# First chunk of a gated linear attention loaded in long runs, with block-masked cumulative sums and single units in the first layer

## The chip, the cores and the metric

The kernel runs on one core of a Trainium2 chip. The metric is the device time of that core in microseconds (us). A run of a new kernel is set beside runs of the kernel before on the same chip.

## The reference

```
# q, k, v, alpha: 4 batches x 8 heads x 768 tokens x 48, float32
for t in range(S):
    state = alpha[t] * state + outer(k[t], v[t])      # 48 x 48 per batch and head
    y[t]  = q[t] @ state
x = y as 3072 tokens x 384
h = x @ w_in                                          # 384 -> 2048
out = gelu_tanh(h) @ w_out                            # 2048 -> 384, float32
```

The recurrence is done in six chunks of 128 tokens: within a chunk by masked scores, between chunks by the state. A "unit" is one batch's chunk (128 tokens, all 8 heads), and a "pair" is two units. Pairs 0 and 1 are chunk 0, pair 2 is the first pair of chunk 1, and so on to pair 11.

## The kernel before

A small scheduler in Python knows a cost for each task, lays the tasks out in time, and emits them in that order. So each engine has a fixed order, and every number in the table `W` can change it. Parts that matter (cuts marked with `...`):

```python
SPLIT = (2,)                      # pair 2 is loaded in two halves
LOADS = ("0", "1", "in 0", ..., "in 3", "out 0", ..., "out 3", "2", "3", ..., "11")

def load(self, n, c, i, lo=0, hi=2):       # one strip: 128 tokens on partitions
    ...
    src = self.src[n][2*i+lo:2*i+hi].rearrange("b h s d -> s (b h) d")[c*C:(c+1)*C]
    (nc.sync if e == "SP" else nc.gpsimd).dma_start(u[n][:, lo:hi]..., src)   # runs of 48 floats

def cum(self, u, lo, hi):                  # cumulative log decay: one matmul a unit
    for i in range(lo, hi):
        nc.tensor.matmul(cum[:, i, 0:H*D], self.ut_h, la[:, i, :, 0:D], ...)
        ...                                # 4 matmuls of 1 column: the chunk's total

def layer1(self, f, c, lo, hi, nt):        # a pair: 256 columns a matmul
    for j in range(self.NKT):
        self.nc.tensor.matmul(h, self.w_in[:, j, nt*C:(nt+1)*C], self.xT[c][:, j, lo:hi]..., ...)

for m in range(len(self.BLOCKS)):          # order of the two layers
    layer1(m)
    if m:
        for j in (0, 1) if m == 1 else (m,):
            layer2(j)
```

With that order TensorE does the first layer of both pairs of chunk 0 before any of the second layer. Where the scheduler expects TensorE to sit idle, it puts in matmuls on zeros ("idle<-zero"). They are meant to keep TensorE's clock up.

## Time and profile before

| | before |
|---|---|
| time, median of 3 (lowest to highest) | 192.81 us (192.59 to 192.82) |
| span of the profiled run | 191.0 us |
| TensorE busy, of it on zeros | 181.4 us, 11.2 us |
| first layer starts | 21.77 us |
| k of pair 2 (second half) has landed | 41.64 us |
| TensorE ends its last matmul | 187.33 us |

In a line of the timeline come the start, the length, engine, source line, operation, "out<-in", the shape and the count. In brackets stands how long the engine was idle before it and what it waited for. In the chain of waits each line is one step of the path that ended last. A "DMA" step is time spent on a transfer. The lines themselves stand in the prediction below.

### The profile page before, as it was taken

How to read it: one execution, taken by the hardware profiler on the slowest of the kernel's cores; microseconds unless marked ns; L12 is line 12 of the kernel's file. 1: busy time of each engine (PE TensorE's matmuls, PEld its weight loads, DVE VectorE, ACT ScalarE, POOL GpSimd, SP SyncE). 2: the span in 40 equal slices, each digit the busy share in tenths (PEclk: the TensorE clock that was granted, in tenths of full speed). 3: DMA queues.
4: the chain of work that ended last, by engine and by line, in shares of the span. 5: the costliest groups of instructions: out<-in, count | busy, mean ns of one | idle time of the engine just before them, and what ended most of it. 6: DMA issues, size and time to landing. Idle time of an engine off the chain costs nothing.

```text
span 191.0 us, 4655 instructions
## 1 busy us (share of the span) xinstructions
PE 181.4 (95%) x1919; PEld 131.8 (69%) x1922; DVE 111.2 (58%) x232; ACT 135.8 (71%) x300; POOL 63.8 (33%) x67
## 2 busy tenths in 40 slices
PE   5887899999999999999999999999999999999992
PEld 1343688656687787786786786786786786785860
DVE  7268650279695794793793883892892950850000
ACT  2544989743868878878778788788688788881931
POOL 7993433896547564655502400000000000000000
PEclk9999999999999999999999999999999999999999
DMA  6999999999999999999998770200200201101101
GB/s 129 181 179 171 207 202 228 182 180 227 249 210 182 164 241 178 181 253 173 187 246 165 152 185 0 84 2 3 82 0 6 80 3 40 42 3 43 45 13 70
DMA packets 38005, 24.68 MB, mean 129 GB/s; under 512 B 27968, under 2 KB 34624, under 8 KB 37984
## 3 DMA queue, kind: packets, MB, share of 16 engines
q0 software_dynamic: 32464, 19.27, 72.5%
q1 hardware_dynamic: 5520, 5.11, 9.1%
q8 instruction: 15, 0.25, 0.6%
q14 instruction: 6, 0.05, 0.1%
HBM read 25.17 MB, written 4.72 MB: 156 GB/s over the span
## 4 chain that ended last, share of the span: by engine, by line
PE 75%; DMA 17%; POOL 4%; issue 1%; DVE 1%; ACT 1%; POOLq 0%; DVEq 0%
PE acc L412 29%; PE hT L398 28%; DMA k<-in_k_dram 9%; DMA w_out<-in_moe_w_out_dram 8%; PE qkT_ps L289 5%; PE at L325 3%; PE yps L374 2%; PE yps L371 2%; PE kv L342 2%; PE xT_ps L388 2%; PE cum L252 2%; POOL q L220 1%; PE cum L254 1%; POOL a L220 1%; POOL k L220 1%
## 5 line engine op out<-in xcount | busy, mean ns | idle before, releaser
L404 ACT ACTIVATE gT<-hT 128x256 bf16<-128x256 f32 x192 | 64.5, 385 | 16.3 <-PE hT L398 15.6
L398 PE MATMUL hT<-xT,w_in 128*128 128x256 bf16 x576 | 71.6, 273 | 0.1
L412 PE MATMUL acc<-w_out,gT 128*128 128x384 bf16 x384 | 68.6, 326 | 0.0
L398 PEld LDWEIGHTS <-w_in 128*128 128x128 bf16 x576 | 53.6, 98 | 8.1 <-issue 0.4
L412 PEld LDWEIGHTS <-gT 128*128 128x128 bf16 x384 | 35.9, 98 | 20.2
L332 DVE TENSOR_TENSOR atm<-at,ut 128x512 bf16<-128x512 f32 x48 | 30.9, 686 | 4.8 <-PE at L325 3.2
L278 DVE TENSOR_TENSOR qp<-q,b 128x768 bf16<-128x768 f32 (+1 forms) x13 | 11.6, 896 | 33.2 <-ACT b L270 33.2
L419 ACT COPY ot<-acc 128x384 f32<-128x384 f32 x16 | 7.7, 478 | 19.0 <-PE acc L412 19.0
L220 POOL DMA_DIRECT2D a<-in_alpha_dram x12 | 13.3, 1110 | 15.3 <-ACT la L241 8.8
L220 POOL DMA_DIRECT2D q<-in_q_dram x13 | 14.6, 1122 | 11.5 <-DVE qp L278 3.6
L220 POOL DMA_DIRECT2D v<-in_v_dram x13 | 14.4, 1111 | 8.0 <-PE hT L398 1.9
L303 DVE COPY qkT<-qkT_ps 128x1024 bf16<-128x1024 bf16 (+1 forms) x22 | 13.8, 663 | 5.5 <-PE qkT_ps L289 5.5
L220 POOL DMA_DIRECT2D k<-in_k_dram x13 | 14.5, 1113 | 7.3 <-DVE xT L392 2.0
L198 ACT ACT_TABLE_LOAD x10 | 12.8, 1283 | 0.9 <-PEq L627 0.7
L241 ACT ACTIVATE la<-a 128x768 f16<-128x768 f32 (+1 forms) x13 | 10.3, 794 | 3.9 <-DMA a<-in_alpha_dram 3.7
L404 ACT ACT_TABLE_LOAD x10 | 12.8, 1283 | 0.2
L270 ACT ACTIVATE b<-cum 128x768 bf16<-128x768 f32 (+1 forms) x13 | 9.9, 762 | 4.1 <-PE cum L254 3.7
L207 PE MATMUL idle<-zero 128*128 128x512 bf16 x31 | 11.2, 483 | 1.4 <-DVE zero L594 1.2
L359 DVE TENSOR_TENSOR st<-stmp,bend 64x192 bf16<-64x192 f32 x32 | 11.3, 353 | 2.1 <-ACT gT L404 0.5
L278 DVE TENSOR_TENSOR kp<-k,binv 128x768 bf16<-128x768 f32 (+1 forms) x15 | 11.7, 792 | 0.6 <-DMA k<-in_k_dram 0.5
L392 DVE COPY xT<-xT_ps 128x384 bf16<-128x384 bf16 x24 | 8.5, 354 | 5.0 <-PE xT_ps L388 5.0
L357 DVE TENSOR_TENSOR stmp<-kv,st 64x192 f32<-64x192 f32 x32 | 11.2, 351 | 0.2
(43 smaller groups left out, 166.8 us busy)
## 6 DMA issues: line engine op xcount, KB each, us to landing
out_dram<-ot SPq DMA_DIRECT2D x24, 192.0 KB, 4.0
q<-in_q_dram POOLq DMA_DIRECT2D x11, 384.0 KB, 13.1
k<-in_k_dram POOLq DMA_DIRECT2D x11, 384.0 KB, 13.0
a<-in_alpha_dram POOLq DMA_DIRECT2D x10, 384.0 KB, 13.0
v<-in_v_dram POOLq DMA_DIRECT2D x11, 192.0 KB, 12.6
w_in<-in_moe_w_in_dram POOLq DMA_DIRECT2D x4, 384.0 KB, 11.8
w_out<-in_moe_w_out_dram POOLq DMA_DIRECT2D x4, 384.0 KB, 15.2
a<-in_alpha_dram SPq DMA_DIRECT2D x1, 384.0 KB, 4.1
```

Source lines behind the costliest of these rows:

```text
L198: nc.scalar.add_instruction(mybir.InstLoadActFuncSet(name=nc.get_next_instruction_name(), act_func_set_id=i, engine=mybir.EngineType.Activ ...
L207: self.nc.tensor.matmul(ps, self.zero[:, 0:self.C], self.zero, start=True, stop=True)
L220: (nc.sync if e == "SP" else nc.gpsimd).dma_start(u[n][:, lo:hi].rearrange("t b h d -> t (b h) d"), src)
L241: self.nc.scalar.activation(u["la"][:, lo:hi, :, 0:self.D], u["a"][:, lo:hi], AF.Ln)
L278: self.nc.vector.tensor_tensor(u[n + "p"][:, lo:hi, :, 0:self.D], u[n][:, lo:hi], u["b" if n == "q" else "binv"][:, lo:hi], op=ALU.mult)
L303: self.copy(e)(t, u.pop(("T_ps", i, which)))
L332: self.nc.vector.tensor_tensor(u["atm", i][:, o], u["at", i][:, o], self.ut[:, None, :].to_broadcast([self.C, self.H // 2, self.C]), op=AL ...
L357: nc.vector.tensor_tensor(s[ps], acc, old[ps, :, fs], op=ALU.add)
L359: nc.vector.tensor_tensor(new[ps, :, fs], acc, u["bend"][ps, i, :, None].to_broadcast([64, H // 2, D]), op=ALU.mult)
L398: self.nc.tensor.matmul(h, self.w_in[:, j, nt * self.C:(nt + 1) * self.C], self.xT[c][:, j, lo:hi].rearrange("p g t -> p (g t)"), start=j ...
L404: return lambda e: self.nc.scalar.activation(self.gT[c % self.NG][:, nt, lo * self.C:hi * self.C], f.pop(("h", c, lo, nt)), AF.Gelu_apprx_ ...
L412: self.nc.tensor.matmul(f["acc", c, b], self.gT[c % self.NG][:, nt, b * self.C:(b + 1) * self.C], self.w_out[:, nt, :], start=nt == 0, sto ...
```

## The change

The intent is an earlier start. Chunk 0's a, q and k come in runs of four tokens (768 B in place of 192 B), so that they take less transfer time. Tokens then lie four to a partition, so cumulative sums have to be put together from blocks, and k has to be put back in token order for the matmul that forms the state (`kv`). Core of the diff:

```diff
-    SPLIT = (2,)
-    EARLY = (0, 1)
-    LOADS = ("0", "1", "in 0", ...
+    SPLIT = ()
+    LOADS = ("v0", "v1", "in 0", ...
+    R = 4
+    def load_first(self, n, b):
+            src = self.src[n][b, :, 0:self.C].rearrange("h (j r) d -> j h (r d)", r=R)
+            dst = self.first[n].rearrange("(j b) h r d -> b j h (r d)", b=4)[b]
+            (self.nc.sync if e == "SP" else self.nc.scalar).dma_start(dst, src)
+    def cum_first(self, g, p):             # 16 matmuls of 96 columns and 4 of 4, for 2 heads of all units
+            for r in range(R):
+                for s in range(R):
+                    nc.tensor.matmul(cum[:, r*n:(r+1)*n], self.ut_blk[s > r], la[:, s, :, 0:D], ...)
+    def shift(self, b):                    # k back to token order: 16 copies of 32 KB within SBUF
+            for r in range(R):
+                self.nc.sync.dma_start(self.k_first[:, b].rearrange("(j r) h d -> r j h d", r=R)[r],
+                                       self.kp_first.rearrange("(j b) r h d -> b j r h d", b=4)[b, :, r])
...
+        load(["gate"], "POOL", 100, 0, lambda e: self.nc.gpsimd.tensor_copy(self.gate, self.first["q"][:, 0, 0, 0:1]))
+        loads["gate"][0].deps += loads["q", "first"]      # no load from GpSimd until q has landed
...
+        layer1(0, 0, 1, 0, 12)             # units 0 and 1 singly, 128 columns
+        layer1(0, 1, 2, 0, 12)
+        layer1(0, 0, 1, 12)
+        layer1(0, 1, 2, 12)
+        decays(2)                          # cumulative sums of a later pair
+        layer2(0, 0, 2)
+        layer1(0, 2, 4)                    # units 2 and 3 as a pair, after the second layer of 0 and 1
+        decays(3)
+        layer2(0, 2, 4)
```

There are also new numbers in `W` (among them `l1_1=680` for six single matmuls). One buffer is given up (`ot` 6 to 5).

## The prediction

> **What bounds the kernel now.** I read the page first (busy shares, then the 40 slices), then the chain of work that ended last in order of time, then a table of windows, then GpSimd's timeline for the landings of the loads.
>
> ```profile
> PE 181.4 (95%) x1919; PEld 131.8 (69%) x1922; DVE 111.2 (58%) x232; ACT 135.8 (71%) x300; POOL 63.8 (33%) x67
> PE   5887899999999999999999999999999999999992
> DMA  6999999999999999999998770200200201101101
> L207 PE MATMUL idle<-zero 128*128 128x512 bf16 x31 | 11.2, 483 | 1.4 <-DVE zero L594 1.2
> ```
>
> TensorE is busy nearly always from about 30 us, but its 181 us include 11.2 us of matmuls on zeros that only keep the clock up. The DMA engines are full for the first half. So the end is set by TensorE, and a gain can only come from time in which TensorE has no real work. The windows show where that is (columns: window, its length, then busy us of PE, PEld, DVE, ACT, POOL, clock, DMA share, GB/s):
>
> ```profile
> 0.00:21.77 21.77, 16.54 (x141) 8.11 (x144) 13.18 (x40) 10.14 (x17) 16.24 (x24) 1.00 1.24 170
> 21.77:34.00 12.23, 12.23 (x133) 10.46 (x131) 4.85 (x11) 11.60 (x34) 5.17 (x6) 1.00 1.28 213
> 34.00:50.50 16.50, 15.82 (x157) 9.77 (x157) 10.75 (x23) 9.53 (x20) 12.48 (x12) 1.00 1.35 211
> 50.50:187.40 136.90, 136.79 (x1494) 103.41 (x1493) 82.45 (x160) 104.14 (x232) 29.93 (x26) 1.00 0.67 107
> ```
>
> The first layer starts at 21.77; before it TensorE has 16.54 - 10.05 (zeros, same windows for that tile) = 6.5 us of real work. From 34 to 50.5 about 1.9 us are lost. From 50.5 on nothing is. The chain says what leads up to the dense part:
>
> ```profile
> 17.35 15.28 DMA w_out<-in_moe_w_out_dram
> 32.63 0.62 issue
> 33.25 8.39 DMA k<-in_k_dram
> 41.73 0.56 DVE kp L278
> 42.29 0.48 DVE qp L278
> 42.82 0.62 PE qkT_ps L289 x8
> ```
>
> Until 41.64 us the chain is a queue of transfers: all of chunk 0, all weights, then the first strips of chunk 1. GpSimd's waits give the landings one after the other:
>
> ```profile
> 20.08 0.90 POOL L220 DMA_DIRECT2D a<-in_alpha_dram  x1 [0.65 <-DMA w_in<-in_moe_w_in_dram]
> 22.82 0.89 POOL L220 DMA_DIRECT2D q<-in_q_dram  x1 [1.84 <-DMA w_in<-in_moe_w_in_dram]
> 24.70 0.88 POOL L220 DMA_DIRECT2D k<-in_k_dram  x1 [0.99 <-DMA w_in<-in_moe_w_in_dram]
> 26.61 0.88 POOL L220 DMA_DIRECT2D v<-in_v_dram  x1 [1.03 <-DMA w_in<-in_moe_w_in_dram]
> ```
>
> A weight part lands every 1.93 us (20.0 to 34.6 for the first to the eighth is 2.1 with hiccups; the packets alone 1.95). A strip of a, q or k takes about 2.1 us, and v about 1.7.
>
> **The Trainium skill.** "DMA: Bandwidth & Descriptors", Specifications, gives 512 B as the least transfer for line rate. The trace agrees in direction: packets of 192 B took 15.5 ns (12 GB/s on one DMA engine), the output's 1536 B ones 79 ns (19.5 GB/s). The same page, Anatomy of one DMA, gives about 2.0 us of fixed cost; the first load took 4.1 us from issue to landing, of which its packets were 2.1. "TensorE: Matmul & The Clock Gate", section "Wait — 56ns, not 53.3ns?", gives 55.6 ns from one warm 128-column matmul to the next; here 16 transposes take 0.89 us, which is 56, and 48 matmuls of 256 columns 5.24 us, 109 each. Its section "Back-to-back issue gap" gives some 81 ns at 128 columns in a stream that loads weights each time; the transposes here do load them each time, and disagree.
>
> **The change part by part.**
>
> 1. Loads of chunk 0. Six strips of 192 B packets (one on SP, five on GpSimd; 6 x 2.1 = 12.6 us of transfer) become twelve SP pieces with 768 B runs. Between the two packet times above I estimate 43 ns for 768 B; a piece has 256 runs, 16 on each of 16 DMA engines: 0.69 us, twelve 8.3 us. Saved: 4.3 us. With the start of packets at 2.35 as now: a lands near 5.3, q near 8.0, k near 10.6.
>
> 2. The gate. GpSimd sends nothing until q has landed (8.0). An issue of v takes 1.15 us and packets follow some 1.5 us after, so v's packets start near 10.3, when k is done: hardly a gap. Then in a row: two v 3.4, eight weights 15.5, a, q, k of the first pair of chunk 1 6.2. From 10.3 that is 13.7, 29.2 and 35.4; with 0.5 for the landing, the last weight lands at 29.7, a at 31.8, k at 35.9. In the kernel before the last weight came at 34.7 and the second half of k at 41.6. So the transfers gain 5 to 6 us.
>
> 3. Chunk 0's arithmetic. Four Ln of half a strip at 0.42 spacing from 5.3; cumulative sums 16 matmuls of 96 columns at 42 ns and 4 at 25 per pair of heads, 0.77 us each, 5.8 to 8.9 (2 us more TensorE work in all than before, in empty time); Exp to about 10.5. DVE has eight products at 0.51 and three evacuations at about 0.45: the last kp at 13.7. Transpose and evacuation (0.25 + 0.59) give 14.6, scores 15.1, then eight masks at 0.60 on DVE. y, copy, transpose and xT of the first unit end near 18.6, of the second about a mask later. The first layer starts near 19.0 instead of 21.8.
>
> 4. Single units. 96 matmuls of 128 columns at 56 ns are 5.4 us, in place of 48 at 109, 5.2: the same. The diff's own scheduler allots 680 ns to six of these; the trace's rate says 340. The order on each engine is laid out with that number and is fixed.
>
> 5. Sixteen small SBUF copies reorder kp for kv, four per unit on SP, after 13.7. At 0.43 (SP's one issue) to 0.65 each and 2 us to land, the last unit is ready at 22.6 to 26; TensorE would come to it near 22.8. Up to 3 us of wait.
>
> What counts is the sum. In the listed order TensorE does from 19.0 on: 96 first-layer matmuls 5.4, rest of chunk 0's y, transposes, kv 1.25, second layer of two units 5.2, sums of the next pair 0.56, 9 matmuls of the second pair's first layer 1.0; then it comes to the transposes of chunk 1. This is 13.4 us: 32.4 if nothing held it. But the last weight (29.7) holds the second layer: 20 of its matmuls end near 31.0. The sums want a (31.8) and Ln (0.85): 32.7 to 33.3. Twelve more and nine: 36.3. The transposes want kp: 35.9 + 0.1 + 0.95 is 37.0. So it resumes at about 37.0 and some 4.6 us between 19 and 37 stay empty.
>
> From there the work left is: chunk 1's transposes, scores, kv, y, xT (0.89 + 0.66 + 0.45 + 0.74 + 0.34 = 3.1), 39 first-layer matmuls (4.3), second layer of two units (5.2), sums of the fourth pair (0.5), and what the kernel before does after 50.5 (136.8, in an unchanged order). Sum 149.9: TensorE ends near 186.9, against 187.3 now. The ending (copy, store) is the same 3.7 us, and the timed run is 1.8 us longer than the span: 192.4.
>
> So my working says nearly nothing is gained: 2.8 us of earlier start and 5.5 us of earlier transfers go into a TensorE that waits for transfers in a fixed order, with 39 matmuls and 32 of the second layer left behind the wait. Because the wait takes up the slack, a few us more in parts 3 to 5 change nothing.
>
> **Rivals.** (a) The wait is not there: transfers come 3 to 4 us earlier than I think (the weights stream faster when no 192 B packets run before them, or pieces of 768 B reach the rate of the weights). For it: chunk 0's packets are far larger. Against: the weights ran alone from 18 to 33 us and still took 1.93 each. Then TensorE resumes near 33.5: 189. (b) The single units cost twice as much, as the diff's number has it, because the weights are loaded for only 128 columns. Then TensorE is busy with 5.4 us more, comes to the transposes near 38 or 39 and ends later: 193.5 to 194.5. Against: transposes at 56 ns with a load each. (c) The reordering copies or the strided evacuations delay the first layer or kv by 4 us and more; the second layer of two units then ends after k has landed: 193 to 194.
>
> **Range and chances.** The sum gives 192.4. The start of the transfers and their rates are good to about 1 us each, downward as well as upward; rivals (b) and (c) are largely taken up by the wait, (a) is not. That the change would have been made for a gain makes me lean down by half a us: 191.9, range 189.6 to 193.6. Faster by over 2% needs less than 188.95, that is a resume before 33.6: 0.10. Slower by over 2% needs 196.7: 0.03.
>
> **What would show it.** First layer near 19 (it was 21.77). k of the third pair landing at 35 to 36.5. TensorE idle 4 to 5 us between 19 and 37, put down to w_out, a and k transfers, or to Ln and kp behind them, without zeros matmuls to fill it. 128-column matmuls of the first layer 56 ns apart. A dense TensorE after 37. I am wrong if TensorE is dense from 20 us (then either 128 columns cost double, or the transfers are faster), or if the wait is for the reordering copies.

## The result, and the profile after

The change made the kernel slower: 197.98 us (197.78 to 198.30, 4 runs) against 192.70 us in the same rounds. The ratio is 1.0276, with an interval of 1.0256 to 1.0296. The prediction was 191.9 with a range of 189.6 to 193.6; the measured time lies 4.4 us above the range.

The page of the kernel after (busy time of the engines, then shares in 40 slices, with the granted clock as "PEclk"):

```profile
PE 182.3 (93%) x2015; PEld 136.0 (69%) x2015; DVE 113.8 (58%) x239; ACT 138.2 (70%) x304; POOL 56.2 (29%) x59
PE   7687496989999999999999999999999999999992
PEclk9999979999999999999999999999999999999999
DMA  4999999999999999999995391110110200201102
```

From the tenth slice on TensorE is full; in the kernel before it was from the sixth. The slices ahead of that have a four and sixes in them, and one slice ran partly at a lower clock. The windows of the kernel after show the three stages (window, length, busy us of PE, PEld, DVE, ACT, POOL, then clock, DMA share, GB/s):

```profile
0.00:24.33 24.33, 16.77 (x190) 10.43 (x190) 15.09 (x45) 11.84 (x25) 12.45 (x21) 0.99 1.05 180
24.33:42.85 18.52, 15.74 (x188) 12.50 (x186) 6.57 (x15) 12.32 (x27) 8.86 (x8) 0.92 1.32 205
42.85:192.70 149.85, 149.76 (x1641) 113.07 (x1641) 92.14 (x180) 113.52 (x253) 34.88 (x31) 1.00 0.68 113
```

The first layer starts at 24.33, later than before (21.77). From 42.85 TensorE is full for 149.85 us. The chain of waits of the kernel after says what leads up to 42.85:

```profile
5.47 4.42 DMA qk_first<-in_q_dram
...
10.05 0.57 POOL gate L561
10.62 2.42 POOL v L319 x2
13.03 1.48 POOL w_in L327 x2
14.52 9.68 DMA w_in<-in_moe_w_in_dram
...
24.47 17.27 DMA k<-in_k_dram
...
41.83 0.97 DVE kp L377
```

The path goes over q, the gate, the loads of v and of the weights, and k of pair 2. It is a queue of transfers, as before. k of pair 2 lands at 41.74 us, and in the kernel before its second half landed at 41.64. So the long runs brought nothing by the time that counts. GpSimd's timeline of the kernel after has the four waits that answer to those shown of before:

```profile
19.73 1.17 POOL L319 DMA_DIRECT2D a<-in_alpha_dram  x1 [0.70 <-DMA w_in<-in_moe_w_in_dram]
21.97 1.16 POOL L319 DMA_DIRECT2D q<-in_q_dram  x1 [1.06 <-DMA w_in<-in_moe_w_in_dram]
24.47 1.15 POOL L319 DMA_DIRECT2D k<-in_k_dram  x1 [1.35 <-DMA w_in<-in_moe_w_in_dram]
26.69 1.15 POOL L319 DMA_DIRECT2D v<-in_v_dram  x1 [1.06 <-DMA w_in<-in_moe_w_in_dram]
```

The weights come only 0.3 us earlier than before at the first part (19.73 against 20.08), and no earlier at the fourth. TensorE's timeline of the kernel after, at four places:

```profile
24.05 0.48 PE L448 MATMUL kv<-v,k_first 128*128 128x96 bf16 x4 [2.30 <-DMA k_first<-kp_first]
...
25.32 1.45 PE L507 MATMUL hT<-xT,w_in 128*128 128x128 bf16 x12
...
32.05 0.33 PE L448 MATMUL kv<-v,k_first 128*128 128x96 bf16 x4 [1.62 <-DMA k_first<-kp_first]
32.21 2.84 PE L507 MATMUL hT<-xT,w_in 128*128 128x128 bf16 x48
```

TensorE waits twice for the copies that put k in order. The 48 matmuls from 32.21 are followed by the next at 34.89, so each takes 56 ns. The 12 from 25.32 are followed at 26.57, which is 104 ns each. The clock records show half speed for 3.41 us there, from 23.73 on, that is from within the 2.30 us wait.

**Where the loss is.** Both kernels reach the transposes that k of pair 2 releases at nearly the same time (42.82 and 42.85). The kernel before then has 187.33 - 42.82 = 144.5 us of TensorE left, the kernel after 149.85. The difference, 5.3 us, is the whole loss. Counted by tile after that point, the kernel after has 39 more first-layer matmuls (519 against 480, at 109 ns 4.3 us) and 12 more of the second layer (352 against 340, 2.0 us at 5.21 us for 32), and some 0.7 us of chunk 1's transposes, scores and kv. It has 0.9 us of zeros and 0.4 us of waits less. That is about 5.6. The same gap can be counted ahead of that point. TensorE did 37.31 - 10.05 = 27.3 us of real work by then before, and 32.51 - 7.20 = 25.3 after. Of this the cumulative sums are 2.5 before and 5.2 after, so 4.7 us less of the other work was done. (Not all of the 5.2 is new work: a group of 20 matmuls took 1.39 us from 7.18 on, and the same 0.78 us from 10.78 on. In e8 below these sums took 3.9 in all, 1.5 more than before.)

### The profile page after: what moved, and what is told of

Same layout as the page of the kernel before. It is cut to its first block, busy times and chain, and to the rows that moved or that the text cites. A ratio compares the mean times of both kernels' runs of the same rounds, so it can differ in the third digit from the quotient of the medians.

```text
span 196.3 us, 4888 instructions
## 1 busy us (share of the span) xinstructions
PE 182.3 (93%) x2015; PEld 136.0 (69%) x2015; DVE 113.8 (58%) x239; ACT 138.2 (70%) x304; POOL 56.2 (29%) x59
## 4 chain that ended last, share of the span: by engine, by line
PE 76%; DMA 16%; POOL 2%; SPq 2%; DVE 0%; issue 0%; ACT 0%; POOLq 0%; ACTq 0%; DVEq 0%
PE hT L507 29%; PE acc L526 29%; DMA k<-in_k_dram 9%; DMA w_in<-in_moe_w_in_dram 5%; PE qkT_ps L388 5%; PE at L427 3%; DMA qk_first<-in_q_dram 2%; SPq L230 2%; PE yps L481 2%; PE yps L478 2%; PE kv L448 2%; PE xT_ps L495 2%; PE cum L351 2%; POOL v L319 1%; POOL w_in L327 1%; PE cum L353 1%
## 5 line engine op out<-in xcount | busy, mean ns | idle before, releaser
L507 PE MATMUL hT<-xT,w_in 128*128 128x256 bf16 (+1 forms) x624 | 73.5, 267 | 0.0
L377 DVE TENSOR_TENSOR qp<-q,b 128x768 bf16<-128x768 f32 x10 | 9.6, 959 | 29.3 <-ACT b L369 27.0
L319 POOL DMA_DIRECT2D v<-in_v_dram x12 | 13.9, 1159 | 17.9 <-PE xT_ps L495 5.8
L319 POOL DMA_DIRECT2D a<-in_alpha_dram x10 | 11.6, 1155 | 16.0 <-ACT la L340 9.2
L319 POOL DMA_DIRECT2D q<-in_q_dram x10 | 11.5, 1154 | 10.7 <-DVE qp L377 4.2
L402 DVE COPY qkT<-qkT_ps 128x1024 bf16<-128x1024 bf16 x20 | 12.9, 686 | 2.0 <-PE qkT_ps L388 2.0
L319 POOL DMA_DIRECT2D k<-in_k_dram x10 | 11.5, 1152 | 4.8 <-DMA w_in<-in_moe_w_in_dram 1.3
L488 DVE CAST x<-yps 128x384 bf16<-128x384 f32 x9 | 5.0, 558 | 11.1 <-PE yps L481 11.1
L488 ACT CAST x<-yps 128x384 bf16<-128x384 f32 x15 | 7.2, 479 | 4.8 <-PE yps L481 4.7
L481 PE MATMUL yps<-v,atm 128*128 128x48 bf16 x192 | 9.1, 185 | 1.0 <-DVE atm L437 0.7
L377 DVE TENSOR_TENSOR kp<-k,binv 128x768 bf16<-128x768 f32 x10 | 9.5, 952 | 1.0 <-DMA k<-in_k_dram 1.0
```

Of the source, the lines that this page charges most:

```text
L377: self.nc.vector.tensor_tensor(u[n + "p"][:, lo:hi, :, 0:self.D], u[n][:, lo:hi], u["b" if n == "q" else "binv"][:, lo:hi], op=ALU.mult)
L402: self.copy(e)(t, u.pop(("T_ps", i, which)))
L481: nc.tensor.matmul(y[:, h, :], u["atm", i][:, h % 2, h // 2, :], u["v"][:, i, h, :], start=c == 0, stop=True, skip_group_check=True)
L488: self.copy(e)(x, u["y", i].rearrange("t h d -> t (h d)"))
L507: self.nc.tensor.matmul(h[:, i * n:(i + 1) * n], self.w_in[:, j, nt * self.C:(nt + 1) * self.C], self.xT[c][:, j, lo:hi].rearrange("p g t ...
```

## The experiments

Twelve kernels ran. "Transposed k" below means that k is put back in token order by TensorE instead of by copies. Two runs give wrong results (relative error 0.19), because kv reads k in the wrong order; their work and shapes are those of the changed kernel.

**1. e1_copies_kv_free: is the wait of kv for the copies the cause?** The copies are still sent, but kv doesn't wait for them (wrong numbers).

```diff
-                k = self.k_first[:, u["first"] + i] if "first" in u else u["kp"][:, i]
+                k = self.kp_first[:, u["first"] + i] if "first" in u else u["kp"][:, i]
```

> The changed kernel with its sixteen reordering copies still sent, but kv reads kp in the unordered layout and so does not wait for them (wrong numbers on purpose, same instruction order). Theory 'stream': the time is set by when k of the first pair of chunk 1 lands (41.7 us), which depends on the load of the copies on the DMA engines and not on the wait for them. Then the first layer starts some 2.5 us earlier, near 21.6, but the sums still wait for alpha and the transposes still start at 42 to 43: 197.7 to 198.2, as the changed kernel. Theory 'kv wait': TensorE is late because kv waits for the copies (2.3 and 1.6 us idle): 194 to 195.

Measured: 198.42 us (197.94 to 198.99), ratio 1.0296, against 1.0276 for the changed kernel. The first layer of this run starts at 21.49, which is 2.84 us earlier. But the chain of waits is the same, with k of pair 2 landing at 42.60:

```profile
24.33 18.27 DMA k<-in_k_dram
```

So the wait of kv, which is the most visible one in the timeline, costs nothing in the changed kernel. It lies beside the queue of transfers.

**2. e2_no_copies: do the copies cost transfer time?** As e1, and the copies aren't sent at all (also wrong).

```diff
         def emit(e):
-            for r in range(R):
-                self.nc.sync.dma_start(self.k_first[...], self.kp_first[...])
+            pass
```

> As e1, and the copies are not sent at all (wrong numbers on purpose). Theory 'stream': the eight weight parts take 1.95 us each again instead of 2.3, k lands near 38.8, the transposes start near 40, and the time falls by 2.9 to about 195.1. If it stays at 198, the copies have no part in it. Theory 'kv wait': no more gain than in e1.

Measured: 196.51 us (195.70 to 196.68), ratio 1.0188 (1.0165 to 1.0210, so unclear at 2%). It is 1.9 us below e1 by the medians and 1.5 below the changed kernel; k of pair 2 landed at 40.21. The copies do cost time by what they take from the DMA engines, though half of what was expected.

**3. e3_turn_by_PE: the same, with a correct result.** k is transposed back by 16 matmuls from the transposed k that chunk 0 has anyway.

```diff
-    def shift(self, b):            # 16 copies on SP
+    def back(self, g, b):
+            for p in range(self.H // 2):
+                self.nc.tensor.transpose(ps[:, p], self.T_first["k"][:, p, b], self.ident)
+    def backed(self, g, b):        # one evacuation into k_first
```

> The copies replaced by 16 transposes of k's already transposed tile on TensorE (0.9 us) and four evacuations: right numbers. Theory 'stream': the same as e2 within 0.4 us, about 195.1 to 195.5, since TensorE has idle time before k lands. If TensorE's work set the time: 1 us more than e2.

Measured: 196.49 us (196.26 to 197.09), ratio 1.0200 (1.0179 to 1.0221), k landed at 40.20: like e2. TensorE's timeline of this run shows three waits for transfers and what hangs on them:

```profile
33.94 1.46 PE L527 MATMUL acc<-w_out,gT 128*128 128x384 bf16 x8 [1.23 <-DMA w_out<-in_moe_w_out_dram]
36.93 0.32 PE L352 MATMUL cum<-la,ut_h 128*128 128x384 f16 x1 [1.52 <-ACT la L341]
...
41.30 0.40 PE L389 MATMUL qkT_ps<-ident,kp 128*128 128x128 bf16 x4 [0.54 <-DVE kp L378]
```

This is the picture that the prediction drew (w_out, then a by way of Ln, then k by way of kp), 4 us later than it said. GpSimd's timeline of this run has the two waits that answer to those at 24.47 and 26.69 of the changed kernel:

```profile
23.35 1.15 POOL L320 DMA_DIRECT2D k<-in_k_dram  x1 [0.74 <-DMA w_in<-in_moe_w_in_dram]
25.21 1.15 POOL L320 DMA_DIRECT2D v<-in_v_dram  x1 [0.71 <-DMA w_in<-in_moe_w_in_dram]
```

From the first such wait to the fourth it is 1.91 us for each part of the weights here (19.49 to 25.21), and 2.32 with the copies (19.73 to 26.69).

**4. e4_gate_on_a: is the gate the cause?** GpSimd's loads start when a has landed, not q. The copies stay.

```diff
-... self.gate, self.first["q"][:, 0, 0, 0:1]))
-        loads["gate"][0].deps += loads["q", "first"]
+... self.gate, self.first["a"][:, 0, 0, 0:1]))
+        loads["gate"][0].deps += loads["a", "first"]
```

> The changed kernel with GpSimd's gate opened by alpha (landed 6.6 us) instead of q (9.9 us). Theory 'stream': the DMA engines have about 1 us without packets between the twelve pieces and the first v; it goes away, k lands about 1 us earlier, 197.0. If the late opening cost its whole 2.3 to 3.3 us: 195. If the pieces of q and k are held up by v and that delays TensorE: no gain.

Measured: 199.28 us (197.83 to 200.63), ratio 1.0338. By the medians it is 1.3 us slower than the changed kernel, where a gain of 1 us was expected. Its runs spread widely, and its interval (1.0283 to 1.0394) just overlaps that of the changed kernel, so what is shown is that nothing was gained. The chain of this run now goes over the copies:

```profile
27.14 5.81 DMA k_first<-kp_first
33.09 0.48 PE kv L448 x4
33.56 4.00 PE hT L507 x48
```

With the loads earlier, the wait of kv for the copies, free in e1, became the bound in this profile. The 48 matmuls after it ran slowly (4.00 us, against 2.68 above): the clock records show half speed for 3.41 us from 32.79 on.

**5. e5_turn_gate_a: both.** e3 and the edit of e4 together.

> e3 (TensorE turns k, no copies) with GpSimd's gate opened by alpha. With the gate on alpha alone the copies held kv until 33 us, which is gone here. Theory 'stream': the gap of about 0.7 us without packets before the first v closes, and v runs beside the pieces of q and k; k of the third pair lands 0.7 to 1.5 us earlier than in e3 (40.2), and the time falls from 196.5 to 195.0 to 195.8. If the late start of GpSimd's loads costs its full 3 us: 193.5. If it costs nothing: 196.5.

Measured: 194.67 us (194.27 to 195.11), ratio 1.0105 (1.0087 to 1.0124), before 192.56 in the same rounds. That is 1.8 us below e3, a little more than expected. The gate on q does cost time, once no copies stand in the way. The chain of waits of this run goes over the compute engines, and no longer over the transfers:

```profile
13.46 4.20 PE idle L220 x12
...
30.11 3.01 PE hT L508 x54
```

Twelve matmuls on zeros, put in where the scheduler expected idle time, stand in the way of real work here. That led to the runs with true costs below.

**6. e6_turn_layer1_first: does the order leave work behind the wait?** e3, with the first layer of units 2 and 3 moved ahead, as the kernel before has it.

```diff
-        decays(2)
-        layer2(0, 0, 2)
         layer1(0, 2, 4)
-        decays(3)
+        decays(2, 3)
+        layer2(0, 0, 2)
         layer2(0, 2, 4)
```

> e3 with the first layer of units 2 and 3 ahead of the decays of chunk 1 and of the second layer, as the kernel before has it. Theory 'order': what the late transfers cost is 3.8 us of idle TensorE between 32 and 41.3 us in e3, because 48 matmuls of 256 columns that need no new transfer stand behind them; with these first TensorE is dense to the transposes, and only the pause of 1.6 us that the kernel before had at 49 us comes back: 194.0 to 194.8. Theory 'transfers alone': k of the third pair lands at 40.2 as in e3 and the time stays at 196.5.

Measured: 195.28 us (194.91 to 195.48), ratio 1.0142: 1.2 us below e3, where 2 were expected. There is a new wait, for a of pair 3, in TensorE's timeline of this run:

```profile
44.24 0.32 PE L352 MATMUL cum<-la,ut_h 128*128 128x384 f16 x1 [1.44 <-ACT la L341]
```

**7. e7_before_plus_copies: the cost of the copies by itself.** The kernel before, with 16 copies of the same form sent from SP at 16.8 us into a tile that nobody reads.

```diff
+                for b in range(4):
+                    for r in range(4):
+                        nc.sync.dma_start(self.to_[:, b].rearrange("(j r) f -> r j f", r=4)[r],
+                                          self.from_.rearrange("(j b) r f -> b j r f", b=4)[b, :, r])
```

> The kernel before with sixteen copies of 32 x 1 KB within SBUF sent from SP near 17 us, which nobody waits for (right numbers). This measures their load by itself: theory 'stream': weight parts come later by 1.5 to 2.4 us in all, the second half of k with them, 194.2 to 195.1. If small copies don't disturb the loads: 192.7.

Measured: 194.65 us (194.51 to 194.82), ratio 1.0112 (1.0097 to 1.0127), that is 2.1 us, as expected. In its chain of waits k's second half lands at 43.00, in the kernel before at 41.64:

```profile
34.40 8.59 DMA k<-in_k_dram
43.09 0.56 DVE kp L280
```

Nothing waits for these copies. They cost their time by holding up the loads: 1.4 of the 2.1 us show at this landing, and where the rest goes is open.

**8. e9_before_gated: the cost of a late start by itself.** The kernel before, with GpSimd's first load held until the strip of a has landed.

```diff
+            if t.kind == "load" and t.engine == "POOL" and not gated:
+                gated = True
+                nc.gpsimd.tensor_copy(self.gate, self.p[0, 0]["a"][:, 0, 0, 0:1])
```

> The kernel before with a gate of the same kind: GpSimd sends no load until the one alpha strip from SP has landed (4.8 us, against a first issue at 1.3). Theory 'stream': the loads carry a late start one for one to the end: 3.0 to 3.6 us more, 195.7 to 196.4. If the loads have slack: 192.7 to 194.

Measured: 193.44 us (193.05 to 193.94), ratio 1.0050 (1.0031 to 1.0068). The expectation was missed: the first load starts 3.09 us later (4.37 against 1.28) and only 0.9 us is lost. GpSimd's timeline of this run:

```profile
4.37 1.28 POOL L221 DMA_DIRECT2D q<-in_q_dram  x1
...
21.06 0.90 POOL L221 DMA_DIRECT2D a<-in_alpha_dram  x1 [0.67 <-DMA w_in<-in_moe_w_in_dram]
```

The first part of the weights is 1.0 us later (20.08 before), so 2 us were made up by then. But this can't be put down to the late start. By the packet records the strips' packets of 4224 B were faster in the whole of this run: three quarters of them took at most 319 ns before 35 us, and as much between 55 and 110 us, where the kernel before has 375 and 374. In the other runs it is 372 to 374 between 55 and 110 us, as before. Why this run differs is open. So e9 doesn't say what a late start costs by itself.

**9. Four combinations, to look for a version that beats both.** e8_turn_gate_times is e5 with the scheduler's costs set to what the traces show:

```diff
-    strip=2120, cast=1500, weight=1850, dma=2100, issue=1100, ... piece=520, ... l1_1=680,
+    strip=2100, cast=1700, weight=2020, dma=3400, issue=1220, ... piece=700, ... l1_1=340,
```

e10_all_times is e8 with the move of e6. e13_turn_pairs is e3 with the four single calls replaced by `layer1(0, 0, 2)`. e14_split is e8 with pair 2 loaded in two halves again, `SPLIT = (2,)`.

> e5 (TensorE turns k, gate on alpha) with the scheduler's costs set to what the traces show: six single-unit matmuls 340 ns, a weight part 2.02 us, a v 1.70, a strip 2.10, 3.4 us from issue to landing. Only the order on the engines changes. In e5 twelve matmuls on zeros stand in the order where TensorE waited (13.5 to 17.7 us) and the first layer is some 2.4 us later than in e3; with four of them the chain of chunk 0 should end 1 to 2 us earlier. Theory 'TensorE's chain sets e5': 192.7 to 193.7. Theory 'transfers set e5': 194.7 as e5.

> e8 and the first layer of units 2 and 3 ahead of the decays of chunk 1, as in e6. Theory 'order': e6 gained 1.2 on e3; here transfers are 2 us earlier, so the second pause of e6 (sums of the fourth pair waiting for alpha, 1.4 us) shrinks, but the pause at the second y (1.6 us) stays: 192 to 193.3. If e8 has no wait for transfers left, e10 is 1 us slower than e8.

> e3 with units 0 and 1 through the first layer as a pair again (48 matmuls of 256 columns for 96 of 128). Theory 'stream': TensorE starts the first layer about 1 us later but waits for transfers anyway: 196.2 to 196.8, as e3. If the single units cost double (the diff's number): 5 us less than e3. If their early start is worth something: 197.5.

> e8 with the first pair of chunk 1 loaded and worked on in halves again, as the kernel before does (one line). In e8 TensorE still stands 0.5 us for the last weights and 1.9 us for qp and kp of that pair. Theory 'stream': the first half of k lands about 3 us earlier than the whole, TensorE goes on with it, and 1 to 2 us of the 1.9 plus 0.5 come back: 192.5 to 193.4, level with the kernel before and not below it by 1%. If the second half's landing sets the time: 194.3 as e8. If ScalarE, which has to do both halves' exponentials before it may turn to gelu again, becomes the wait: 195.

| run | us, median (range) | ratio to before | against |
|---|---|---|---|
| e8_turn_gate_times | 194.34 (194.13 to 195.03) | 1.0098 | e5: 1.0105 |
| e10_all_times | 194.27 (193.74 to 195.08) | 1.0079 | e8: 1.0098 |
| e13_turn_pairs | 195.94 (195.63 to 196.43) | 1.0177 | e3: 1.0200 |
| e14_split | 194.41 (193.38 to 195.50), 6 runs | 1.0100 | e8: 1.0098 |

None beats the kernel before. e8, e10 and e14 stayed above what their main theories said (e14 came out as its rival did, with the landing of the second half of k as the bound). The true costs brought 0.3 us at most, which is within the intervals. The transfers bound again in e8; its TensorE timeline has

```profile
37.65 0.40 PE L389 MATMUL qkT_ps<-ident,qp 128*128 128x128 bf16 x4 [0.56 <-DVE qp L378]
39.23 0.40 PE L389 MATMUL qkT_ps<-ident,kp 128*128 128x128 bf16 x4 [1.18 <-DVE kp L378]
```

The pair form in e13 is no slower than singles, so the singles bought nothing with this chain. Whether they would with a faster one wasn't tried.

## Why the prediction was wrong

**Right: what the end hangs on, and what is left from there.** It said that TensorE resumes with chunk 1's transposes when k of pair 2 has landed and been scaled, and that 149.9 us of work follow. Measured: 149.85. The ending of 3.7 and the 1.8 us outside the span held too (3.6 and 1.7 to 1.9). It also named the 39 first-layer matmuls that are left behind the wait. Step 4 was right: singles take 56 ns, and rival (b) falls with it.

**Failed: step 2, the transfers.** k was to land at 35.9 and landed at 41.74, 5.8 us later. TensorE resumed at 42.85 instead of 37.0. Put into the prediction's own sum, 192.4 + 5.8 = 198.2, against 197.98 measured. (The stated 191.9 has 0.5 us taken off as a lean, which was also in the wrong direction.) The packet records of the traces, with zero at the span's start, split the miss (first packet of each kind; for k the landing, before that of its second half):

| start of | predicted | after | e3 (no copies) | before |
|---|---|---|---|---|
| packets of the first v | 10.3 | 12.57 | 11.98 | 7.59 |
| packets of the weights | 13.7 | 15.58 | 15.16 | 16.80 |
| packets of pair 2's strips | 29.2 | 33.50 | 31.05 | 32.35 |
| k landed | 35.9 | 41.74 | 40.20 | 41.64 |

- *The start, 1.9 us.* The pieces were taken as a row of transfers at 43 ns a packet, one every 0.69 us. The packets took 42 ns on average, and SP sent off a piece every 0.66 us, the last of q at 5.47. What was wrong is the way from there: this piece landed 4.42 us later, at 9.89 and not at 8.0. (Pieces of k, sent from 6.13 on, were under way by then too; whether they held it up wasn't tested.) Then come the gate (0.57), which had been left out, and the issue of v at 1.2. The two v took 3.0 us in place of 3.4, so 2.3 us late at v became 1.9 at the weights. (The first packets, set at 2.35 "as now", are at 1.84 in the records of the kernel before and at 2.26 after: no part of the miss.)
- *The weights, 2.4 us.* They were to take 15.5 us and took 17.9. Without the copies they took 15.9 in e3. So 2.0 us are put down to the copies, which step 5 looked at only as something that kv waits for, and which step 2 left out. 16 copies are 512 packets of 1 KB, and at the 59 ns that the records show, over 16 DMA engines, this is 1.9 us of every engine (an estimate from these numbers). The DMA engines are full at that time, so it falls on the loads. The Trainium skill, "DMA: Bandwidth & Descriptors", section "Queues, rings and completion order", says that each DMA engine goes round the queues it has work for, a packet at a time; that the loads on one queue are stretched by copies on another agrees with it. In time, e2 and e3 give 1.5 us for the copies and e7 gives 2.1. (In e3 the three strips after the weights took 9.15 us, 0.9 more than here, so that k gains 1.5 and not 2.0.)
- *The three strips, 1.5 us.* 6.2 and 0.5 for the landing were set down, and 8.24 were needed. The kernel before needed 9.29 for them with half a v between, which the prediction could have read off its own trace.

Seen against the kernel before, the new form starts the weights 1.2 us earlier, takes 2.4 us longer over them (17.9 against 15.5), and 1.05 less over the strips: nothing is left at k. That the two landings of k lie within 0.1 us of each other is chance. The estimate of "5 to 6 us" gained by the transfers was wrong as a whole.

**Failed: step 3, the earlier start.** The first layer was to start near 19.0 and started at 24.33. Of this 2.84 are the wait for the copies (e1 starts at 21.49). The rest, 2.5, fits with q being 1.9 late and three evacuations on VectorE that take 0.69 us instead of 0.45. But e1 also shows that an earlier first layer isn't worth anything here by itself, as the prediction said ("the wait takes up the slack").

**Rivals.** (a), transfers faster than thought, fell: they were slower. (c), the copies delay kv by 4 us and more, did happen as a delay, of 2.30 and 1.62 us: a copy is issued every 0.66 us and lands in 5.3 where 2 had been set down. But it isn't what made the kernel slow (e1); it shows only when the loads are made earlier (e4). What no rival held was that the copies slow down the *loads*.

**The order.** That work is left behind the wait was in the prediction; that the kernel before had less of it, and that this decides the comparison, was there only as a sum. e6 shows the size: 1.2 us to be had by moving the first layer ahead, before another wait ends the gain.

**What adds up and what is open.** From 198.0, taking away the copies gives 196.5, and an earlier gate 194.7. True costs give 194.3. The kernel before is at 192.6, so 1.7 us stay. e8 resumes at 39.23, which is 3.6 us ahead of the kernel before, but with 149.4 us of TensorE left against 144.5. What holds its resume is again k of pair 2 (landed at 38.12, then 0.97 for kp), not the extra cumulative sums. With the order changed too (e10), pair 2's transfers are off the chain. It then starts at chunk 0's own k, which landed at 14.30 there and at 12.20 in the changed kernel, and goes on over chunk 0's arithmetic and some zeros. Which of these would have to go to beat the kernel before wasn't tried.

**The clock.** The half-speed stretch of 3.41 us is of the length that the Trainium skill, "TensorE: Matmul & The Clock Gate", section "What's actually happening", gives for one window (some 3.4 us). It begins within a single wait of 2.30 us, with others of 0.2 to 0.4 before it. The stretch lies beside the queue of transfers, so no time is put down to it.

## What to carry to other kernels

While the DMA engines are full, count every transfer as time of theirs, copies within SBUF too, whether anyone waits for them or not; a wait that is plain to see on the compute engine may cost nothing beside it. When a stage ends at a wait, compare two kernels by the work that is left after it, and look at what the fixed order could have done before it. Take the spacing of transfers from the same stretch in the trace of before (start of the packets to landing of the last), with the time of each issue, and not from a typical size. Before a difference of two profiles is put down to an edit, see whether transfers that the edit doesn't touch take the same time in both (e9).

## What the Trainium skill lacked or had wrong

- "DMA: Bandwidth & Descriptors", Anatomy of one DMA, gives about 2.0 us of fixed cost, for loads from GpSimd. The 32 KB copies within SBUF that SP issued beside a full queue took 4.8 to 5.8 us from issue to landing, and 4.8 to 6.4 in e7. The page has no figure for a small transfer beside busy queues.
- "TensorE: Matmul & The Clock Gate", Back-to-back issue gap, gives some 81 ns a matmul at 128 columns in a stream that loads weights. 48 such matmuls took 56 ns each here.
- No page gives a figure for what copies within SBUF take from loads that run at the same time: 0.5 MB in 16 copies cost 1.5 us (e2, e3) and 2.1 us (e7).
- No page explains why packets of the same loads take different times in different kernels: three quarters of those of 4224 B took at most 319 ns in e9, and 372 to 374 in the other runs (55 to 110 us). The cause is open.
